# A fused attention, mixture-of-experts and dense kernel: attention paced ahead of the MoE, unsplit probabilities in the first chunk, the third MoE run backwards through its weights

## Chip, cores and metric

The kernel runs on one core of one Trainium2 chip. The metric is the device time of one execution in microseconds; lower is better. Engines are named as in the profile: PE is TensorE, DVE is VectorE, ACT is ScalarE, POOL is GpSimd, SP is the engine on which every DMA of this kernel is issued.

## What is computed

```python
# q, k, v: 2 batches, 8 heads, 768 positions, 64 wide; proj: 64 x 6
q_bucket, k_bucket = sign bits of q @ proj, k @ proj      # 6 bits make a bucket
scores = where(q_bucket == k_bucket, q @ k.T / 8, -1e9)
attn = softmax(scores) @ v                                # per batch and head
x = attn, heads side by side                              # 1536 tokens x 512
p = domain_probs / sum(domain_probs)
moe = sum over 4 experts e of p[:, e] * (relu(x @ w1[e]) @ w2[e])   # 512 -> 1024 -> 512
h = moe @ w_in                                            # 512 -> 1024
solu = h * softmax(h)
ln = (solu - mean) / sqrt(var + 1e-6) * g_ln
out = ln @ w_out                                          # 1024 -> 512
```

w_in, w_out and g_ln follow the inputs' double precision; the kernel decodes w_in and w_out from 64-bit words on the chip.

## The kernel before

The 1536 tokens are cut into four chunks of 384 (three tiles of 128). Chunks 0 and 1 belong to batch 0, chunks 2 and 3 to batch 1. For each chunk there is an attention (8 heads with 3 rows of 128 queries each) and a MoE of 32 slots; slot s has an A step (`moe_a`, L1312: 12 products of 384 columns against w1) and a B step (`moe_b`, L1363: 9 products of 512 columns against w2). At the end `dense` (L1453) does the last part for twelve tiles.

Precision is got by splitting: a value becomes a high and a low part, and a product is done as three. In the first chunk's attention and MoE the parts are f32r (a reduced fp32), later fp16. Weights arrive by DMA in `wra` (w1) and `wrb` (w2), 512 KB each, and are split into `wsa`, `wsb` by one instruction on ACT, DVE or POOL and one on DVE (`Stream.split`, L1245). Every chunk loads and splits all 16 + 16 pieces again; from the second chunk on the split parts go round a ring of 4 pairs for each kind (`ws16_r`, L521).

The first chunk's attention (`attn_first`, L937) stands alone at the start. Heads 0 to 5 normalise each row of probabilities, split it (`xh`, `xl`, `t`, `hha`, `hxa`) and multiply both parts with both parts of v: 12 f32r products for a head. Heads 6 and 7 (`h >= FH`) are *full*: probabilities are neither normalised nor split, transposed as they are into fp32 tiles (`ln`, `y`), multiplied in 6 fp32 products with a v tile (`wrb`) whose other half is ones, so that the sums come out beside the result, and divided afterwards (`av_out`, ratio, L906).

The attention of chunk c+1 (`attn_steps`, L1124) is mixed into the MoE of chunk c. A row (L1141 to L1153) does scores on PE, the maximum on DVE, the exponential on ACT (`p<-PS,sm`), scaling, a split into `hl`, and a DMA transpose into `t` or `t320h`; after three rows `av_mm` multiplies with v and `av_out` makes the chunk's input `xh`, `xl`. The first chunk of a batch also projects all k of that batch (`proj_steps(c, True)`, L1128), which takes the place of 9 steps. `Fill` (L1518) hands out steps by a rate per slot: chunk 1 in 22 slots, then, restarted two slots before each MoE's end, 31 slots for chunk 2 (50 steps, the k projection among them) and for chunk 3 (41 steps).

The program is recorded first. What is then issued is set by three tables: `ORDER` (which recorded operation comes next, over all engines), `FORMS` (which engine takes an operation that has a choice) and `BANKS` (which PSUM bank). `Recorder.emit` (L383) follows them; nothing is decided at run time, and each engine takes its instructions in that order.

Of the kernel before, what the change touches and what calls it, by code (L numbers as in the profile page):

```python
# [401 lines left out]
def lsh_attention_moe_solu(  # L402
# [17 lines left out]
    R = S // 128  # L420
# [14 lines left out]
    NR = 16  # L435
    LQ = 2 * D + NR
    LW = 128

    LA = 2
    GS = 2  # L440
    FH = 6
    LD = 1
    LB = 3
    DI = 2
    BM, BS, BE, BQ = 100, 150, 100, 50
    OUT0 = 4
    DBOOST = 0
# [473 lines left out]
    def x_tiles(c):  # L921
# [3 lines left out]
        if c:  # L925
            xT[c] = lower
# [591 lines left out]
    class Fill:  # L1518
# [6 lines left out]
        def start(self, c, slots):  # L1525
            for _ in self.it:
                pass
# [83 lines left out]
```

## Time and profile before

| | |
|---|---|
| time, median of 3 runs | 879.75 us (876.97 to 881.87) |
| the profiled execution's own time | 878.72 us |
| its span, first to last instruction | 876.6 us |
| PE busy | 832.7 us, 95% |
| DVE, ACT, POOL busy | 715.3, 489.6, 306.5 us |
| chain that ended last | PE 70%, DVE 9%, DMA 9%, issue 4%, ACT 3%, POOL 3% |
| DMA | 180.42 MB, mean 206 GB/s |

The profile gives, for one execution, when each engine was busy and what ended its idle time. All operations go through one recording helper, so nearly all stand under one line, L397; groups are told apart by the names of the tiles that they write and read (`out<-in`). A busy PE need not be PE at its peak, and the granted clock of PE is listed beside it.

### The profile page before, as it was taken

What the parts mean: (1) busy time and instruction counts of PE and PEld (TensorE: products, weight loads), DVE (VectorE), ACT (ScalarE), POOL (GpSimd) and SP (SyncE); (2) the same over time, 40 slices, a digit from 0 to 9 for tenths busy, and PEclk for the clock granted to TensorE, in tenths of its full rate; (3) what the DMA queues carried; (4) which work ended last, traced back from release to release, by engine and by line L of the source; (5) the groups of instructions that cost most, each with busy time, mean ns of one, the idle gap of its engine ahead of it and who ended that gap; (6) DMA issues with size and microseconds to landing.
All of it is one profiled execution on the core that took longest, in us unless ns stands there. A gap on an engine that the chain in (4) does not pass through costs nothing.

```text
span 876.6 us, 13313 instructions
## 1 busy us (share of the span) xinstructions
PE 832.7 (95%) x4431; PEld 531.4 (61%) x4431; DVE 715.3 (82%) x1476; ACT 489.6 (56%) x894; POOL 306.5 (35%) x325
## 2 busy tenths in 40 slices
PE   6789999999999999999769999999999999999997
PEld 5677789888886555655435555555555555444443
DVE  7978767877888978889978788887888889999872
ACT  4878547676795333667853566586344534443431
POOL 1645552545533131244512243543433221111220
PEclk9999999999999999999969999999999999999999
DMA  7986766998999798899998799999477857234643
GB/s 193 261 202 180 222 205 140 229 238 211 243 241 290 249 261 245 204 268 230 227 191 265 181 277 233 252 242 215 145 248 206 253 194 248 67 80 79 125 97 96
DMA packets 250069, 180.42 MB, mean 206 GB/s; under 512 B 166673, under 2 KB 218257, under 8 KB 250001
## 3 DMA queue, kind: packets, MB, share of 16 engines
q1 hardware_dynamic: 250000, 179.58, 79.4%
q8 instruction: 35, 0.57, 0.3%
q14 instruction: 34, 0.27, 0.1%
HBM read 116.10 MB, written 19.73 MB: 155 GB/s over the span
## 4 chain that ended last, share of the span: by engine, by line
PE 70%; DVE 9%; DMA 9%; issue 4%; ACT 3%; POOL 3%; SPq 1%; POOLq 0%; DVEq 0%; ACTq 0%
PE PS L397 70%; DMA t<-hl 5%; ACT p L397 2%; DVE sm L397 2%; DMA t320h<-hl 1%; POOL hl L397 1%; SPq L397 1%; DVE hl L397 1%; DVE st L397 1%; DVE p L397 1%; DMA wrb<-in_moe_w_dram 1%; DVE ln L397 1%; DVE wsa0h L397 1%; DVE xp L397 0%; DMA qB<-qD 0%
## 5 line engine op out<-in xcount | busy, mean ns | idle before, releaser
L397 ACT ACTIVATE p<-PS,sm 128x768 f32<-128x768 f32 x96 | 94.9, 989 | 34.9 <-DVE sm L397 16.8
L397 DVE TENSOR_REDUCE sm<-PS 128x1 f32<-128x768 f32 x96 | 90.8, 950 | 20.2 <-PE PS L397 19.1
L397 PEld LDWEIGHTS <-wsa1h 128*128 128x128 f16 x576 | 55.7, 98 | 42.1 <-issue 3.7
L397 PEld LDWEIGHTS <-wsa0h 128*128 128x128 f16 x576 | 55.6, 98 | 39.8 <-issue 1.6
L397 POOL TENSOR_SCALAR sm<-sm 128x1 f32<-128x1 f32 x97 | 34.3, 355 | 107.3 <-DVE sm L397 52.4
L397 PE MATMUL PS<-xh,wsa 128*128 128x384 f32 x256 | 68.8, 336 | 0.0
L397 PE MATMUL PS<-kB,qB 80*128 80x384 f32 x192 | 66.1, 344 | 2.0 <-DMA qB<-wsb 1.4
L397 PE MATMUL PS<-xh1h,wsa1h 128*128 128x384 f16 x256 | 67.0, 326 | 0.9 <-DVE y L397 0.9
L397 PE MATMUL PS<-xh1h,wsa0h 128*128 128x384 f16 x256 | 66.7, 326 | 0.0
L397 ACT ACTIVATE hha0h<-PS 128x384 f16<-128x384 f32 (+1 forms) x66 | 31.9, 489 | 58.4 <-PE PS L397 55.7
L397 POOL TENSOR_TENSOR hl<-p,hl 128x768 f16<-128x768 f32 x25 | 42.6, 1704 | 58.1 <-DVE hl L397 28.6
L397 PEld LDWEIGHTS <-hha0h 128*128 128x128 f16 x400 | 36.8, 98 | 40.5 <-issue 3.7
L397 PE MATMUL PS<-kC,qC 128*128 128x384 f32 x144 | 56.1, 390 | 5.0 <-ACT p L397 4.8
L397 PE MATMUL PS<-wsb0h,hha0h 128*128 128x512 f16 x200 | 59.7, 380 | 0.0
L397 PE MATMUL PS<-wsb1h,hha0h 128*128 128x512 f16 x200 | 59.6, 380 | 0.0
L397 DVE TENSOR_TENSOR hl<-p,hl 128x768 f16<-128x768 f32 x47 | 45.7, 973 | 10.1 <-ACT hl L397 5.1
L397 ACT ACTIVATE p<-p,sm 128x768 f32<-128x768 f32 x47 | 43.6, 931 | 15.9 <-DVE sm L397 15.6
L397 POOL TENSOR_SCALAR ln<-ln 128x512 int32<-128x512 int32 x21 | 23.9, 1136 | 77.0 <-DVE ln L397 69.7
L397 PEld LDWEIGHTS PS<-xh,wsa 128*128 128x128 f32 x256 | 46.6, 188 | 0.4
L397 DVE SCALAR_TENSOR_TENSOR hxa0h<-PS,hha0h 128x384 f16<-128x384 f32 x64 | 34.8, 550 | 10.2 <-ACT hha0h L397 10.1
L397 PE MATMUL PS<-xl,wsa 128*128 128x384 f32 x128 | 43.0, 336 | 0.0
L397 PE MATMUL PS<-wsb,hha 128*128 128x512 f32 x132 | 41.9, 398 | 0.0
(303 smaller groups left out, 2292.7 us busy)
## 6 DMA issues: line engine op xcount, KB each, us to landing
wra<-in_moe_w_dram SPq DMA_DIRECT2D x64, 512.0 KB, 5.1
wrb<-in_moe_w_dram SPq DMA_DIRECT2D x64, 512.0 KB, 4.7
kC<-kD SPq DMA_DIRECT2D x24, 384.0 KB, 4.4
vr<-in_v_dram SPq DMA_DIRECT2D x30, 192.0 KB, 4.0
kB<-kD SPq DMA_DIRECT2D x24, 240.0 KB, 4.8
qD<-stk SPq DMA_DIRECT2D x27, 192.0 KB, 3.2
qC<-qD SPq DMA_DIRECT2D x24, 192.0 KB, 3.9
ln<-in_moe_w_in_dram SPq DMA_DIRECT2D x8, 512.0 KB, 4.5
```

The source lines that it names most:

```text
L397: fn(**{key: self.now(x) for key, x in kw.items()})
```

## The change

- `FULL` holds all eight heads: in the first chunk no probability is normalised or split. The full heads' transposed probabilities now go to the `t` tiles and v to the `hl` (fp16) tiles read as fp32. `av_out` copies the numerators to `xp` and divides two heads at once, on odd heads.
- The k projection of batch 1 moves from the head of chunk 2's attention to the tail of chunk 1's.
- `Fill` follows one table of ends: chunk 1's q projection and attention by slot 22, both projections for chunk 2 by slot 32, chunk 2's attention by slot 55, all of chunk 3's by slot 89 of the first 96.
- The third MoE takes its weights in reverse. The split parts of the last six pieces of each kind stay in SBUF, and the next MoE's first six are those: 6 loads and splits of each kind fewer in the third MoE, and as many in the fourth. The ring grows to 6 pairs; the two new ones lie in `ln` and `ee`.
- The decoding of w_in and w_out begins at slot 4 of the last MoE and is spread to slot 30, since it uses `ln`.
- `ORDER`, `FORMS` and `BANKS` are new throughout.

```diff
 ORDER = """
-3 13 0 1 0 10 28 14 21 14 1 19 9 22 18 9 0 0 16 2 0 15 8 0 26 11 11 12 19 5 10 2 10 9 5 0 12 7 3 12 3 9 5 9 8
...
-    FH = 6
+    FULL = (0, 1, 2, 3, 4, 5, 6, 7)
...
+    x = cuts(ln_r.t[0], 1024) + cuts(ee_r.t[0], 1024)
+    for i in (1, 2):
+        j = 4 * (i - 1)
+        ws16_r[i].t = [(x[j], x[j + 1]), (x[j + 2], x[j + 3])] + ws16_x[i]
...
         if ratio:
             acopy(tmp[m, 0:N], ps[l0:l0 + 64, 0:N], bias=1e-9)
-            V.reciprocal(out=tmp[m, 0:N], in_=tmp[m, 0:N])
-            V.tensor_tensor(out=xp[m, 0:N], in0=ps[m, 0:N], in1=tmp[m, 0:N], op=ALU.mult)
+            copy_by("AV", xp[m, 0:N], ps[m, 0:N])
+            if h % 2 == 1:
+                V.reciprocal(out=tmp[:, 0:N], in_=tmp[:, 0:N])
+                sub_by("VG", xp[:, 0:N], xp[:, 0:N], tmp[:, 0:N], ALU.mult)
...
-            full = h >= FH
+            full = h in FULL
...
     def attn_steps(c):
-        if r0 == 0:
-            yield from proj_steps(c, True, None, a_b, pp_b, stk_r)
...
+        if c + 1 < NC and chunks[c + 1][1] == 0:
+            yield from proj_steps(c + 1, True, None, a_b, pp_b, stk_r)
...
         def split(self, i):
+                if self.ns in self.again:
+                    self.spl[self.ns] = self.spl[self.again[self.ns]]
...
+    KEEP = 6
+    def turned(c, x):
+        return x[::-1] if c == 2 else x
...
+            if c > 1 and len(W1.items) - i1["m", c, turned(c, range(NP))[0]] < KEEP:
+                W1.again[len(W1.items)] = i1["m", c - 1, m]
...
     class Fill:
-        def start(self, c, slots):
...
+        ends = ((NS - 10, H + 1 + H * (NT + 1)), (NS, 2 * H + 2), (2 * NS - 9, H * (NT + 1)), (3 * NS - 7, H + 1 + H * (NT + 1)))
...
-            if c == NC - 1 and s % DI == 0:
+            moe_b(c, s)
+            if c == NC - 1 and s > 3 and (s - 4) * 16 // 26 > (s - 5) * 16 // 26:
                 next(dec_it, 0)
```

The tables' effect shows in the order of instructions. Three places follow, all on PE. The first is head 0's product with v in the first attention (`vs` is v, `wsa,wsb` and `kB,qB` are scores, `idn,p` transposes of probabilities). Before:

```order
L397 MATMUL PS<-kB_126,qB_128 128x384
L397 MATMUL PS<-xh_94,vs_74 128x384 x4
L397 MATMUL PS<-hha_108,vs_74 128x384 x2
L397 MATMUL PS<-xl_96,vs_74 128x384 x4
L397 MATMUL PS<-hxa_110,vs_74 128x384 x2
L397 MATMUL PS<-idn,p_77 128x128 x4
```

With the change (`t` holds the probabilities, `hl` holds v):

```order
L389 MATMUL PS<-kB_126,qB_128 128x384
L389 MATMUL PS<-idn,p_79 128x128 x4
L389 MATMUL PS<-idn,p_77 128x128 x6
L389 MATMUL PS<-t_82,hl_80 128x384 x6
L389 MATMUL PS<-wsa_104,wsb_106 128x384
```

Twelve f32r products became six fp32 products. The second place is the end of batch 1's k projection (`idr,hl` transposes k, `stk,lhs_w` projects it). Before, it is among products of the second MoE (`xh1h,wsa1h`, fp16):

```order
L397 LDWEIGHTS hxa0h
L397 MATMUL PS<-wsb0h,hxa0h 128x512
L397 MATMUL PS<-stk_66,lhs_w 128x384 x2
L397 LDWEIGHTS wsa1h
L397 MATMUL PS<-xh1h,wsa1h 128x384
```

With the change it is among B steps of the first MoE (`wsb,hhb`, f32r):

```order
L389 MATMUL PS<-wsb_106,hhb_109 128x512 x2
L389 MATMUL PS<-wsb_106,hxb_111 128x512
L389 MATMUL PS<-idr,hl_65 128x128 x3
L389 MATMUL PS<-stk_67,lhs_w 128x384 x2
L389 MATMUL PS<-wsb_106,hhb_109 128x512 x2
L389 MATMUL PS<-wsb_106,hxb_111 128x512
L389 MATMUL PS<-stk_66,lhs_w 128x384 x2
```

The projection moved ahead of the whole second MoE. The third place is the end of chunk 2's attention (`t83,vs1h` and `t320h,vs2h` are products with v of heads 5 and 6, the rest is chunk 3's q projection). Before, no product of a MoE stands between them:

```order
L397 MATMUL PS<-t_83,vs1h 128x384
L397 MATMUL PS<-idr,hl_65 128x128 x3
L397 MATMUL PS<-idr,hl_64 128x128 x3
L397 MATMUL PS<-stk_66,lhs_w 128x384
L397 MATMUL PS<-stk_67,lhs_w 128x384
L397 MATMUL PS<-idr,hl_65 128x128 x3
L397 LDWEIGHTS vs2h
L397 MATMUL PS<-t320h,vs2h 128x384
```

With the change, behind head 6's product, B steps of the second MoE (`wsb0h,hha0h`) are still to be done:

```order
L389 MATMUL PS<-t320h,vs2h 128x384
L389 MATMUL PS<-stk_66,lhs_w 128x384
L389 MATMUL PS<-idr,hl_64 128x128 x3
L389 MATMUL PS<-idr,hl_65 128x128 x3
L389 LDWEIGHTS hha0h
L389 MATMUL PS<-wsb0h,hha0h 128x512
L389 LDWEIGHTS hha0h
L389 MATMUL PS<-wsb0h,hha0h 128x512
```

Work of the second MoE was all issued ahead of these products; now some of it is left for PE while the last heads finish, ahead of the third MoE's first product.

## Rows read from the trace of the kernel before

**Rows 1.** The page: span, and part 1, busy time of each engine.
```profile
span 876.6 us, 13313 instructions
PE 832.7 (95%) x4431; PEld 531.4 (61%) x4431; DVE 715.3 (82%) x1476; ACT 489.6 (56%) x894; POOL 306.5 (35%) x325
```

**Rows 2.** Busy time by stage: stretch, length, engines' busy us (instructions), PE clock, DMA, GB/s.
```profile
16.90:95.50 78.60, 66.07 (x374) 54.33 (x372) 66.76 (x140) 61.39 (x136) 41.28 (x70) 0.98 0.79 215
95.50:270.40 174.90, 172.74 (x918) 151.72 (x917) 135.17 (x247) 117.02 (x215) 85.83 (x73) 1.00 0.84 216
270.40:426.50 156.10, 154.03 (x856) 88.36 (x856) 133.43 (x245) 83.97 (x151) 50.44 (x56) 1.00 0.95 252
426.50:462.20 35.70, 22.10 (x106) 14.51 (x106) 28.01 (x55) 21.72 (x47) 11.25 (x17) 0.76 0.92 199
462.20:621.60 159.40, 157.76 (x866) 90.76 (x866) 130.37 (x238) 95.66 (x166) 60.04 (x57) 1.00 0.97 234
621.60:747.60 126.00, 126.00 (x682) 66.56 (x680) 109.78 (x187) 57.52 (x98) 34.98 (x27) 1.00 0.70 219
747.60:876.60 129.00, 124.22 (x580) 56.68 (x578) 99.56 (x341) 44.67 (x70) 19.36 (x13) 1.00 0.40 88
```

**Rows 3.** Waits of PE from 426 to 463 us: total, times, longest.
```profile
PE PS L397 <- DVE xp L397: 5.2, 1, 5.2
PE PS L397 <- ACT p L397: 4.4, 2, 2.8
PE PS L397 <- DMA qD<-stk: 2.5, 1, 2.5
```

**Rows 4.** Groups: the exponential in 270.4:426.5, 426.5:462.2, 462.2:621.6 (x is rows).
```profile
L397 ACT ACTIVATE p<-PS,sm 128x768 f32<-128x768 f32 x17 | 16.8, 987 | 4.2 <-POOL sm L397 2.3 <-DVE sm L397 1.6
...
L397 ACT ACTIVATE p<-PS,sm 128x768 f32<-128x768 f32 x7 | 6.9, 987 | 0.1
...
L397 ACT ACTIVATE p<-PS,sm 128x768 f32<-128x768 f32 x24 | 23.7, 987 | 13.0 <-DVE sm L397 9.1 <-POOL sm L397 1.8 <-DVE hxa0h L397 1.7
```

**Rows 5.** Timeline of PE at 79 us: start, length, instruction, count.
```profile
79.56 2.25 PE L397 MATMUL PS<-t,vs 128*128 128x384 f32 x12
81.64 4.03 PE L397 MATMUL PS<-ln,wrb 128*128 128x384 f32 x12
85.51 2.33 PE L397 MATMUL PS<-idn,p 128*128 128x128 f32 x18
```

**Rows 6.** Waits of PE from 16.9 to 95.5 us: total, times, longest.
```profile
PE PS L397 <- POOL p L397: 3.4, 5, 1.0
PE PS L397 <- ACT p L397: 3.1, 6, 1.1
...
PE PS L397 <- DVE hxa L397: 0.9, 1, 0.9
...
PE PS L397 <- ACT sm L397: 0.6, 1, 0.6
PE PS L397 <- DVE xl L397: 0.6, 1, 0.6
```

**Rows 7.** Groups in 16.9:95.5: busy, mean ns, idle time before.
```profile
L397 POOL TENSOR_SCALAR p<-p,sm 128x768 f32<-128x768 f32 x12 | 10.9, 906 | 9.4 <-DVE sm L397 8.5 <-PE PS L397 0.7
...
L397 DVE TENSOR_TENSOR xl<-PS,xh 128x512 fp32r<-128x512 f32 x9 | 6.1, 682 | 0.1
...
L397 DVE RECIPROCAL tmp<-tmp 64x384 f32<-64x384 f32 x2 | 5.1, 2547 | 1.3 <-ACT tmp L397 1.3
```

**Rows 8.** The page: a weight's second split; a load of w1 and its landing.
```profile
L397 DVE SCALAR_TENSOR_TENSOR wsb1h<-wrb,fit,wsb1h 128x1024 f16<-128x1024 f32 x26 | 35.2, 1356 | 3.4 <-POOL wsb1h L397 1.9 <-ACT wsb1h L397 1.4
...
wra<-in_moe_w_dram SPq DMA_DIRECT2D x64, 512.0 KB, 5.1
...
t<-hl SPq DMA_TRANSPOSE x48, 4.8
```

More of the change, by code (lines that the diff above doesn't have):

```diff
@@ L23 @@
 ORDER = """
[106 rows of a table removed]
[99 rows of a table added]
 """
 FORMS = """
-AGVVGVAGAVVVVAAVAAVAAVVAVAAAAAGAGGAVVVVAGAAGAAGAVAVGAGAGAGGGAGAGAGAAAAGGGAGAGAGVAGAGAAGGGGGVGAGAAVGAAAVVAAAGVA
-AGGVGAAVAVGGAAGAGVAAGVVGGAAAVVGAAAGGAAGGAGVVGVGAGAVAVVAGVAGAVVAVAAVVGGGGVGAGVGAVVAVAAGVAGAGAGAGAAGAAGGVVGVAAVA
-GGGAVGVGAAVAVVVGVVAVGAAVAGVGVVVAGGAGVVAVGAVAVAVAVAAVAVVGVVVAGAGGVAVGVGAVAGGAVAVGVAVAVVAGVAAVVVAVGAGAGVGVVGAAVG
-AAAGGAGVAAVAVAAVVVAGGAVVVGGGAAGVVGVAVVAGVVAVAVAVGVAAGVAGAGAAVAVGVGAAVGAVGGGGAGVAAVAVAAVAVGVVGVGGAGVAGAVVVVAGVG
-AVAGVVAGAVVGVVAGAVAVVGAVVAAVAAGGVAGVAVVAVVAAVVAAGGVGAVAAGAVVAAAAVGAGGAVGAAVAGGVAAVVGVVAVVAVAVAAGAVVVVAVVVGGGGG
@@ L138 @@
-GGVAAGGAAAAGVGAGVVVVGAAVGAAVVAVVAGVVVAVAVAGAAGAGVVVAAAAVGVAGGVVAGGAAAGVAGAVVAAVVGVAVGAGVAGAGVVAVAGAAAAAVGVGVVG
-VGAVGVGVVAGVAGAAVAVAVVAVGAGAGGGAGGAGAVAGAGGVAAGAAAAGGAGAVAGVAAAGGAVGAVVAVAVAGGGVAGVAAVVAVVVAGVVVVVAAGVAGVVVVAV
-VAVAVVVVAAVVVGVVGVVAVVVAVVAGGAGGGVAGVVAAGAAVVVGVVAVAGAVVVVVAAVAVVAAGGVAAGAGAVVVAVVVAAVVAAVGGAAVAGVGVGVAAGGVVGG
-AGGGGVGGGAVAVGGVAAAVAGAGVGVVVGAVVVAAAAAGGVVVAVVGGAAGAGVAGVAGAGVAAAAAGVAGGVVVAVVAAVVAGAGGAAGVAVVVVAVVVAGAVGAGVV
-GGAAGAVVVAVAAGAGVAAGAAVAVAVGGAAVAAAGGAAAAVAAVVVGAAAVAAGGVAAAAAVAAVAAVAGAGGGAVVAVVGAVAAVVGGAGAAGVVVAGGGAVAVVAVA
@@ L143 @@
-A
+GVAVAAVVVAAVAAVAAVAGAAAVVAAAAAVVGAVAAAVVAGAVGVAGVAVAVVVAVAVAGGAVGGVGVAGVGGAVAAVVVAAAGAGAAVVVAAVVVGVVVVGAGVAAAG
+GVGAVAVVAAAGAVVVVGAAGAVGVGVAVGVGAAVVGGVVGGAAGVAVAVAAAVVAVVAVVVAVAAVVAVAAGVVGGGVAVAAVVAGGVVGAAVAVGVAGAAAVGVAVAA
+GGAVVVVAVVVAVGAGAAVGVAGAAAVAGVAAGVGVVVVVAAGVVAVVAVAAVGAAVVVAGGAAAGVGVGAAAGVVAAVAGVVGAGVAAVAAVAAVAVVAAGAAVGVAGA
+GVGAAVVAGAVAGVAGVAAVGVAGVAGVVAVAVGAAVAGVAVAGAGVAVGAAGAVAGAGVVGVAVGVAVAGAGVAGVVGVAAGAGVGVVAGAGVVGGAVAVAVAVGVAGA
+GVGVAGAAGVAAAVVAVVGAGVAVAVAVGAVVVVVVGVVVVAGAGVGVAAAGAGVAAGAGGGGAAVGAAAAVVVAAVAAVAAGAAGAAAAAGVAGAVGVVVAAAGGAVVV
@@ new lines @@
+AVGAGVGGAVGVAVVVGAAAAGGAAVGAGGAAAVGAGVVGVAAGAVAVAGVVAGAGVVGGVVVAAVVAGGVVAVAAGGAGGAAVAVVAGAVAGVGGGAAGAAGVGGGAVA
+GGVAVVVVAAVAVVVGAGVVAVAGVAGVGVGVVGAGAGGAAVVVVGAGAAAVGVAAVGAVVGVVGAVGGVGGGGVGVAVVAVVAGAVVVGAGAGAGVGGGAGAGAGGGGG
+VGGVVAGAAVAVGVAGAGGVGVVGVAGVVAVVAGGGGAGVGVAAGVAVGVGVGGVVAAVGVVAGVAGVVVAGAGVGGVVGAVVGGVAGGAVAGAGVAAVAGVGAGVAGAV
+VAAVVAGVGGAVAAVVGGAGAGVVAGGVVGVAAAAVGVAVVVGVVGVVGGVAVGVGVVVVVAGAAGGAAAGVVAVAVAAGAVVVGAVAAAVAGGAAVAAAAVGAAAAVAA
+AVAAVAVAVAVAAVGAAAVVVGAAAVVVGAGGGVAAAGAGVAGVGVAAVAA
@@ L144 @@
 """
 BANKS = """
-73062064160357612045050120461040726540235742036431020136124061234163021423610432613401423612010263704250767216
-03076234651436521065324635645635634513240365757436446362030621455364346453753763467621321301270231630127367676
-37451340273524574375462146340635634634656103621406346564367464206410204600234523406753213640356456420345731634
-63636513046210367537436436034231607351254735647574325702540143041623673541702645656450135645620546026340326342
-630162410
+52174372354027165406053217317503741604530215626304121064013063464210601241647203606234102360142010754604712147
@@ L152 @@
+54102447536564365401620546345346537546320164326573563543463536346546402163767373637337667376363763653672047163
+73344365436365312065435736543463261452103754357466353655456036214046343674646377365630241635345345450357436521
+36565734634356021403643634534636346561256452012707123653246124130462423534120657205264763545642106462343063206
+235161043
 """
@@ L520, in lsh_attention_moe_solu @@
     hh16_r, hl16x_r = (Ring(0, tiles=cuts(t[1], TM) + cuts(t[0], TM)) for t in (hh_t, hx_t))
-    ws16_r = {}
+    ws16_r, ws16_x = {}, {}
     for i in (1, 2):
@@ L524, in lsh_attention_moe_solu @@
         ws16_r[i] = Ring(0, tiles=[(x[a][2 * j], x[a][2 * j + 1]) for j in range(2) for a in range(2)])
+        ws16_x[i] = ws16_r[i].t
     y_r = Ring(1, [128, NT, DM], F32, "y")
@@ L561, in sub, with sub_by @@
         eng.tensor_tensor(out=out, in0=a, in1=b, op=ALU.subtract)
-    def sub_by(names, out, a, b):
-        rec.add([(name, "tensor_tensor", dict(out=out, in0=a, in1=b, op=ALU.subtract)) for name in names])
+    def sub_by(names, out, a, b, op=ALU.subtract):
+        rec.add([(name, "tensor_tensor", dict(out=out, in0=a, in1=b, op=op)) for name in names])
     def ops_by(names, out, in_, a, b, op0, op1):
@@ L654, in fit_v @@
     def fit_v(b):
-        ts = [t.rearrange("p a r q -> p (a r q)").bitcast(F32)[:, 0:H // 2 * R * D] for t in t16_r.t[0:2]]
+        if b:
+            ts = [t.rearrange("p a r q -> p (a r q)").bitcast(F32)[:, 0:H // 2 * R * D] for t in t16_r.t[0:2]]
+        else:
+            x = ln_r.t[0].rearrange("p a n -> p (a n)")
+            ts = [x[:, i * H // 2 * R * D:(i + 1) * H // 2 * R * D] for i in range(2)]
         for i, t in enumerate(ts):
@@ L921, in x_tiles @@
     def x_tiles(c):
-        xT[c] = x = (xh_r.next(), xl_r.next())
-        lower, upper = (tuple(flat16(t)[:, i * KD * TM:(i + 1) * KD * TM].rearrange("p (k q) -> p k q", k=KD) for t in x) for i in range(2))
-        yT[c] = upper if c < 2 else lower
-        if c:
-            xT[c] = lower
+        x = (xh_r.t[0 if c in (0, 3) else 1], xl_r.t[0 if c in (0, 3) else 1])
+        lower, upper = (
+            tuple(flat16(t)[:, i * KD * TM:(i + 1) * KD * TM].rearrange("p (k q) -> p k q", k=KD) for t in x) for i in range(2)
+        )
+        xT[c], yT[c] = {0: (x, upper), 1: (lower, lower), 2: (upper, upper), 3: (lower, lower)}[c]
     def row(U, rr, sb, E, pr_=p_r):
@@ L1023, in attn_first @@
         vs_f = Ring(0, tiles=vs_r.t[0:2])
-        vp = [t.rearrange("p a n -> p (a n)")[:, 0:S].rearrange("p (r a d) -> p r a d", r=R, a=2) for t in wr_r[2].t]
+        vp = [t.rearrange("p a n -> p (a n)").bitcast(F32).rearrange("p (r a d) -> p r a d", r=R, a=2) for t in hl16_r.t]
         for hi, t in enumerate(vp):
@@ L1043, in unit @@
             hi = h % 2
-            if h >= FH:
+            if h in FULL:
                 vs = vp[hi]
@@ L1065, in attn_first @@
         )
-        cut = lambda x: x.rearrange("p (m q) -> p m q", q=N)
-        fdst = Ring(
-            0,
-            tiles=[
-                [[cut(kf[:, 0:KD * N])], [cut(kf[:, KD * N:R * N])]],
-                [[cut(qf[:, 0:KD * N])], [cut(kf[:, R * N:2 * R * N - KD * N])]],
-            ],
-        )
+        fdst = [t.rearrange("p a r q -> p (a r q)").bitcast(F32).rearrange("p (r q) -> p r q", r=R) for t in t16_r.t[0:2]]
+        fdst = Ring(0, tiles=[[[t[:, 0:KD]], [t[:, KD:R]]] for t in fdst])
         U = unit(0)
@@ L1229, in __init__ @@
             self.of = {}
+            self.again = {}
+            self.tile = {}
             self.nl = 0
@@ L1239, in load @@
             while self.nl <= min(i, len(self.items) - 1):
+                if self.nl in self.again:
+                    self.nl += 1
+                    continue
                 t = self.as_item(wr_r[self.kind].next(), self.nl)
@@ L1246, in split @@
             while self.ns <= min(i, len(self.items) - 1):
+                if self.ns in self.again:
+                    self.spl[self.ns] = self.spl[self.again[self.ns]]
+                    self.tile[self.ns] = self.tile[self.again[self.ns]]
+                    self.ns += 1
+                    if self.ns not in self.again:
+                        ring = ws16_r[self.kind]
+                        ring.t = [self.tile[i] for i in range(self.ns - KEEP, self.ns)]
+                        if self.of[self.ns][0] == NC - 1:
+                            ring.t = [t for t in ring.t if any(t is x for x in ws16_x[self.kind])]
+                        ring.n = 0
+                    continue
                 self.load(self.ns)
@@ L1250, in split @@
                 if c:
-                    w = ws16_r[self.kind].next()
+                    self.tile[self.ns] = w = ws16_r[self.kind].next()
                     w = [x.rearrange("p (a n) -> p a n", a=t.shape[1]) for x in w]
@@ L1271, in lsh_attention_moe_solu, with slot @@
     i1, i2 = {}, {}
+    NP = NS // 2
+    KEEP = 6
+    def turned(c, x):
+        return x[::-1] if c == 2 else x
+    def slot(c, s):
+        return NS - 1 - s if c == 2 else s
     def add_moe1(c, lo, hi):
-        for m in range(lo, hi):
+        for m in turned(c, range(lo, hi)):
             e, fp = divmod(m, NF // 2)
             i1["m", c, m] = len(W1.items)
+            if c > 1 and len(W1.items) - i1["m", c, turned(c, range(NP))[0]] < KEEP:
+                W1.again[len(W1.items)] = i1["m", c - 1, m]
             W1.of[len(W1.items)] = c, m
@@ L1280, in add_moe2 @@
     def add_moe2(c, lo, hi):
-        for m in range(lo, hi):
+        for m in turned(c, range(lo, hi)):
             e, fp = divmod(m, NF // 2)
             i2["m", c, m] = len(W2.items)
+            if c > 1 and len(W2.items) - i2["m", c, turned(c, range(NP))[0]] < KEEP:
+                W2.again[len(W2.items)] = i2["m", c - 1, m]
             W2.of[len(W2.items)] = c, m
             W2.items.append(w2[e][fp * 256:fp * 256 + 256, :].rearrange("(k p) f -> p k f", p=128))
-    NP = NS // 2
     for c in range(NC):
@@ L1312, in moe_a @@
     def moe_a(c, s):
-        m, j = divmod(s, 2)
+        m, j = divmod(slot(c, s), 2)
         i = i1["m", c, m]
@@ L1331, in moe_a @@
         hT["m", c, s] = split_h(ps, N, True, c == 0)
-        if j == 0:
+        if s % 2 == 0:
             W1.split(i + 1)
@@ L1350, in lsh_attention_moe_solu, with y_update @@
     y_t = {}
-    def y_update(c, e, t):
+    def y_update(c, at, e, t):
         b, r0, n = chunks[c]
@@ L1355, in y_update @@
         g = pr[:, b * R + r0 + t, e:e + 1]
-        if e == 0:
+        if at == 0:
             if t == 0:
@@ L1361, in y_update, with moe_b @@
             V.scalar_tensor_tensor(out=y_t[c][:, t], in0=o, scalar=g, in1=y_t[c][:, t], op0=ALU.mult, op1=ALU.add)
-    def moe_b(c, s, more=0):
+    def moe_b(c, s):
         n = chunks[c][2]
-        parts = []
-        for x in range(s, s + more + 1):
-            m, j = divmod(x, 2)
-            parts.append((x, W2.get(i2["m", c, m]), hT.pop(("m", c, x)), j))
-        for tiles in [[t] for t in range(n)] if more else [range(n)]:
-            for x, w, (hh, hl), j in parts:
-                e, fi = divmod(x, NF)
-                mm2(("m", c), tiles, hh, hl, w, j, fi == 0, fi == NF - 1)
-            if fi == NF - 1:
-                for t in tiles:
-                    y_update(c, e, t)
-                    if e == E - 1:
-                        y_fit(c, t)
-        m, j = divmod(s + more, 2)
-        i = i2["m", c, m]
-        if j == 0:
+        m, j = divmod(slot(c, s), 2)
+        i = i2["m", c, m]
+        hh, hl = hT.pop(("m", c, s))
+        at, fi = divmod(s, NF)
+        mm2(("m", c), range(n), hh, hl, W2.get(i), j, fi == 0, fi == NF - 1)
+        if fi == NF - 1:
+            for t in range(n):
+                y_update(c, at, slot(c, s) // NF, t)
+                if at == E - 1:
+                    y_fit(c, t)
+        if s % 2 == 0:
             W2.split(min(i + 1, i2["out", 0] - 1))
@@ L1518, in lsh_attention_moe_solu, with __init__, __call__ @@
     class Fill:
-        it = iter(())
-        rate = 0.0
-        due = 0.0
-        def start(self, c, slots):
-            for _ in self.it:
-                pass
-            if c < NC:
-                b, r0, n = chunks[c]
-                self.it = attn_steps(c)
-                self.rate = ((H + 1) * (2 if r0 == 0 else 1) + H * (n + 1)) / slots
-            self.due = 0.0
-        def __call__(self, w=1.0):
-            self.due += self.rate * w
-            while self.due >= 1.0:
-                self.due -= 1.0
+        ends = ((NS - 10, H + 1 + H * (NT + 1)), (NS, 2 * H + 2), (2 * NS - 9, H * (NT + 1)), (3 * NS - 7, H + 1 + H * (NT + 1)))
+        def __init__(self):
+            self.it = (x for c in range(1, NC) for x in attn_steps(c))
+            self.at, self.done = 0, 0
+        def __call__(self):
+            self.at += 1
+            due = first = 0
+            for end, steps in self.ends:
+                due += steps * min(1.0, max(0.0, (self.at - first) / (end - first)))
+                first = end
+            while self.done < int(due + 1e-6):
+                self.done += 1
                 next(self.it, 0)
@@ L1553, in lsh_attention_moe_solu @@
     W2.split(0)
-    fill.start(1, NS - 10)
     for c in range(NC):
@@ L1559, in lsh_attention_moe_solu @@
         for s in range(NS):
-            if s == NS - LA and c + 1 < NC:
-                fill.start(c + 2, NS - 1)
             a_to(c, s + LA + 1)
@@ L1564, in lsh_attention_moe_solu @@
                 a_to(c + 1, s + LA + 1 - NS)
-            fill()
-            if c == NC - 1 and s % DI == 0:
+            if c < NC - 1:
+                fill()
+            moe_b(c, s)
+            if c == NC - 1 and s > 3 and (s - 4) * 16 // 26 > (s - 5) * 16 // 26:
                 next(dec_it, 0)
-            moe_b(c, s)
-            if c == NC - 1 and s == 17:
+            if c == NC - 1 and s == 18:
                 fit_norm(dm[:, 0:8].unsqueeze(1), NM, WA)
```

204 rows, old and new, of the table ORDER are left out of this document.

## Prediction

> **What bounds the kernel now.** I read the page first: PE is busy for 832.7 of 876.6 us, more than any other engine [rows 1]. So the time is PE's work plus the 43.9 us in which PE waits, and an edit counts only if it changes one of the two. Next I cut the span where PE's work changes its kind [rows 2]: the first attention (16.9 to 95.5), the four MoEs (to 270.4, 426.5, then 462.2 to 621.6, and 747.6) and the dense end. The reader is to compare the first number of a row, its length, with the second, PE's busy time. In the second and third MoE rows and in the last MoE they nearly agree: 154.03 of 156.10, 157.76 of 159.40, 126.00 of 126.00. Two rows stand out. The first attention leaves 78.60 - 66.07 = 12.5 us idle. The stretch from 426.5 to 462.2 leaves 35.70 - 22.10 = 13.6 us idle, and there PE's granted clock averages 0.76: it fell from 2.4 to 1.2 GHz for part of the stretch, after its longer idle times, so the same products also took longer.
>
> What is that stretch? It lies between the second MoE's last product and the third MoE's first. The waits [rows 3] name `xp`, `p` and `qD`, all tiles of the attention. The count of exponentials tells how late that attention is [rows 4]: of chunk 2's 24 rows, 17 were done by 426.5 and 7 were left. The third MoE needs all of them. PE has nothing but these rows and chunk 3's q projection to do, and the row chain (maximum, exponential, split, DMA transpose) sets the pace, 35.7 / 7 = 5.1 us for a row. I call the stretch the hole.
>
> **The change, part by part.**
>
> *Attention paced ahead, k projection moved.* If chunk 2's attention ends before the second MoE does, the hole's products lie beside MoE products that are needed anyway. The hole's real work is PE's busy time at full clock: 22.10 x 0.76 = 16.8 us. What goes is 35.7 - 16.8 = 18.9 us. Does it end in time? The third MoE's stretch held 24 rows in 159.4 us with 1.6 us idle [rows 2, 4], 6.6 us a row. The second MoE's stretch gets longer by the hole's work, 156.1 + 16.8 = 172.9 us, less the k projection, which goes to the first MoE; I count some 165 us, in which 24 rows at 6.6 us need 159. That fits, with little to spare, and only because the projections are over when the second MoE begins, as the second place of the order shows. The k projection's loads, stores and transposes go to a stretch with a DMA share of 0.84 instead of 0.95, DVE 77% busy instead of 85% [rows 2]; PE's work in it only changes place, so it costs nothing in the sum. On SP its 8 loads and 8 stores now queue among chunk 1's last transposes, where a late one would delay chunk 1's last rows; MoE work lies behind those, so I charge nothing there. What is late next is the tail of chunk 2: in the new order head 7's product with v has only a few MoE products around it, and a transpose lands 4.8 us after its issue [rows 8]. The nearest wait of that kind took 5.2 us [rows 3]. Bounds are 0 and 5.2 us; nothing speaks for either end, so I take about the middle, 2.5 us.
>
> *Unsplit probabilities.* Six heads go from 12 f32r products to 6 fp32 products. The timeline has both next to each other [rows 5]: 12 f32r products from 79.56 to 81.64 are 2.08 us; 6 fp32 products, shown as 12 records, from 81.64 to 85.51 are 3.87 us. Each head costs PE 1.79 us more, six heads 10.7 us, on the path. The records go at 3.87 / 12 = 0.32 us, so one fp32 product takes 0.645 us. The Trainium skill (FP8 and Floating Point Precision, section TensorE Precision Notes) says that true fp32 takes four passes through the array. By that rule an fp32 product would be four f32r products, 4 x 2.08 / 12 = 0.69 us, and the six heads would cost 6 x (4.16 - 2.08) = 12.5 us. By the rows it is 3.87 / 2.08 x 2 = 3.7 f32r products, so the trace does not quite agree, and the measured 10.7 us stands in the sum.
>
> What it gives back is waits. The removed work is the scaling of 18 rows (906 ns each on POOL), the second copies of the split (682 ns for the larger half on DVE), the split of v, and the row reciprocals [rows 7]. It adds numerator copies and two more reciprocals of 2547 ns (four in place of two, for two heads each) [rows 7]. DVE, ACT and POOL were busy for 66.8, 61.4 and 41.3 us of the 78.6 [rows 2]; none is the bound alone, but PE waited for just these instructions. Of PE's waits those on POOL's `p` (3.4 us), on `hxa` (0.9), `xl` (0.6) and the row scale `sm` (0.6) lose their cause, and about half of those on ACT's `p` (3.1), which is both scaling and exponential [rows 6]: 3.4 + 0.9 + 0.6 + 0.6 + 1.5 = 7.0 us. Bounds: 0, if scores and loads come last instead, and 12.5, all of the idle time. A head's fp32 products also cover 3.87 us of the next rows' chain, which is why I do not go below 7.
>
> *The third MoE backwards.* 24 loads of 512 KB and 24 splits go: 24 x 1.36 = 33 us of DVE and about as much on ACT and POOL, and 24 x 0.5 MB of DMA [rows 8]. I charge nothing for it. In both stretches in which it falls PE was busy for all but 1.6 us [rows 2], so it is off the path; it helps only as slack for the attention's tail. If the cover went, one split of 1.36 us would show at a time. The decoding starts four slots later, as it needs `ln`, and its 16 steps go at the same pace over the same MoE; behind it PE has 126.0 of 126.0 us of its own, and the decode of w_in has still to be over before the dense part. Zero again; above it, at most one step's delay, 126 / 16 = 7.9 us; a gain is excluded since PE is full there.
>
> *Sum.* 876.6 + 10.7 - 7.0 - 18.9 + 2.5 = 863.9 us of span. The profiled execution took 878.72 us for a span of 876.6, 2.1 us more: 866.0 us. It lies 1.0 us under the median of the runs shown, 879.75, well inside their spread, so I leave it at that.
>
> **The rivals.**
>
> *The hole only shrinks* (no change). The row chain in the second MoE needs more than the 6.6 us of the third, since the stretch also ends the projections and reads with a DMA share that was 0.95 already. A delay of 0.4 us a row is 24 x 0.4 = 10 us of hole. Against it: the 7 rows in the hole went at 5.1 us. Time: 866 + 10 = 876 us.
>
> *The chain stays behind PE* (slower). If a row of chunk 2 takes 7.4 us or more beside a full MoE, with one transpose stream, one SP queue and DVE at 85%, the third MoE begins some 24 x 0.8 = 19 us late: the hole is back in full, in whatever place, and the fp32 products are still paid. Time: 866 + 19 = 885 us. It decides at 7.2 us a row, where 24 x 0.6 = 14 us eat up the gain. For it speaks that the order is fixed by tables and one late transpose holds the SP queue for all; against it the 24 rows at 6.6 us in the third MoE with the same engines.
>
> *The first attention becomes PE's own* (faster still). If the long fp32 products hide the whole row chain, all 12.5 us of idle time return and the tail of chunk 2 is covered: 876.6 + 10.7 - 12.5 - 18.9 + 2.1 = 858 us. For it speaks that every side engine loses work; against it that PE there also waited for the loads of `qB` and the exponential, which stay.
>
> *It does nothing that it says* is excluded for the places shown: the order has them moved.
>
> **How the numbers follow.** The forecast (hole closed, part of the first waits returned, 861 to 871 us) gets 0.62, the faster rival 0.16, the shrunken hole 0.15, the slower one 0.07. The likeliest is 866 us. The range goes from 857, just below the faster rival, to 876, the shrunken hole; with no waits returned and the 5.2 us tail the sum is 876.6 + 10.7 - 18.9 + 5.2 + 2.1 = 875.7 us, also its end. A measurement of this kernel can tell about 0.5%, 4.4 us, from no change. Faster than 875.4: 0.62 + 0.16 and a third of the shrunken hole, 0.83. Within: 0.11. Slower than 884.1: 0.06.
>
> **What would show it.** Right: no stretch of over 6 us with PE idle between the second and third MoE; clock 1.00 there; 24 exponentials before the second MoE's last product; fp32 products at 0.32 us a record and the first attention some 4 us longer. Wrong: PE waits on `xp`, `hl` or `t` for over 10 us around the third MoE's start; the first attention over 10 us longer; a new wait on `ln` or on weights at the start of the last MoE or of the dense end.

## The result and the profile after

The changed kernel takes 866.82 us (median of 4 runs, 864.93 to 867.72) against 879.12 us before (now of 4 runs): a ratio of 0.986, 95% interval 0.982 to 0.989. It is faster by 1.4%, clear of the noise, and 866.0 us had been forecast. The profiled execution took 864.93 us for a span of 863.0 us. The page after, span and part 1, against [rows 1]:

```profile
span 863.0 us, 13106 instructions
PE 835.2 (97%) x4431; PEld 528.6 (61%) x4431; DVE 666.6 (77%) x1387; ACT 471.1 (55%) x862; POOL 274.8 (32%) x302
```

PE is busy for 2.5 us more and idle for 16.1 us less: 863.0 - 835.2 = 27.8 us, where it was 876.6 - 832.7 = 43.9. By stage (columns as in [rows 2]; the second MoE's first product is at 276.2 us, the third's at 438.8, the fourth's at 601.1, the dense part's at 724.5):

```profile
16.50:96.70 80.20, 72.75 (x368) 53.34 (x367) 56.83 (x96) 52.76 (x112) 18.57 (x34) 1.00 0.78 211
96.70:276.20 179.50, 178.07 (x958) 155.88 (x957) 144.93 (x263) 127.11 (x238) 81.78 (x76) 1.00 0.90 243
276.20:438.80 162.60, 159.19 (x895) 93.60 (x894) 136.59 (x263) 100.33 (x184) 64.39 (x76) 1.00 0.96 241
425.00:455.00 30.00, 30.00 (x171) 17.52 (x170) 21.50 (x40) 9.65 (x20) 8.02 (x14) 1.00 0.48 128
438.80:601.10 162.30, 160.23 (x874) 91.59 (x873) 117.10 (x217) 80.45 (x145) 58.66 (x69) 1.00 0.75 178
724.50:863.00 138.50, 131.39 (x611) 59.76 (x609) 105.60 (x354) 50.94 (x80) 18.73 (x13) 1.00 0.43 100
```

The fourth line is the place where the hole was: PE is busy for all 30 us at a clock of 1.00, where [rows 2] had 22.1 of 35.7 us at 0.76. The third MoE now starts 11.3 us before the second one's last product ends at 450.1 us. The exponential's group in 276.2:438.8 has all of chunk 2's rows ([rows 4] had 17):

```profile
L389 ACT ACTIVATE p<-PS,sm 128x768 f32<-128x768 f32 x24 | 23.7, 986 | 12.2 <-DVE sm L389 5.8 <-POOL sm L389 4.8 <-POOL hl L389 1.0
```

The first attention has 80.20 - 72.75 = 7.45 us of idle PE, where [rows 2] had 12.5, and 6.7 us more of PE's work. Its waits: `POOL p`, `hxa`, `xl` and `sm` are gone as forecast, while those on ACT's `p` grew from 3.1 us [rows 6] to 4.7:

```profile
PE PS L389 <- ACT p L389: 4.7, 8, 1.0
PE PS L389 <- DMA wsa<-wsa: 1.0, 1, 1.0
PE PS L389 <- DVE xp L389: 0.5, 1, 0.5
```

The timeline of PE shows the six fp32 products (12 records) of two heads, and what follows each:

```profile
65.25 4.04 PE L389 MATMUL PS<-t,hl 128*128 128x384 f32 x12
69.12 1.84 PE L389 MATMUL PS<-idn,p 128*128 128x128 f32 x14
...
72.20 4.03 PE L389 MATMUL PS<-t,hl 128*128 128x384 f32 x12
75.78 0.63 PE L389 MATMUL PS<-wsa,wsb 128*128 128x384 f32 x1
```

From the first start to the last end a head takes 4.03 to 4.04 us, as it did before (4.03 in [rows 5]), and the records follow each other every 0.32 us. From start to the next group's start it is 3.87 us where transposes follow and 3.58 us where a score follows, but that score's record is then 0.63 us long, where one behind another score is 0.34 us: it begins before the fp32 products end. So 3.58 us is no shorter product.

### The profile page after: what moved, and what is told of

Read it like the earlier page. It is cut to its first block, busy times and chain, and to the rows that moved or that the text cites. A ratio compares the mean times of both kernels' runs of the same rounds, so it can differ in the third digit from the quotient of the medians.

```text
span 863.0 us, 13106 instructions
## 1 busy us (share of the span) xinstructions
PE 835.2 (97%) x4431; PEld 528.6 (61%) x4431; DVE 666.6 (77%) x1387; ACT 471.1 (55%) x862; POOL 274.8 (32%) x302
## 4 chain that ended last, share of the span: by engine, by line
PE 71%; DVE 13%; DMA 7%; ACT 4%; issue 2%; SPq 2%; POOL 1%; ACTq 0%; DVEq 0%; POOLq 0%
PE PS L389 71%; DVE sm L389 3%; DVE ln L389 2%; ACT p L389 2%; DVE st L389 2%; DMA t<-hl 2%; SPq L389 2%; DMA qD<-stk 1%; DVE hl L389 1%; DMA xh1h<-hl 1%; POOL sm L389 1%; DMA wra<-in_moe_w_dram 1%; DMA xl0h<-hl 1%; DVE tmp L389 1%; DVE t L389 1%
## 5 line engine op out<-in xcount | busy, mean ns | idle before, releaser
L389 DVE TENSOR_REDUCE sm<-PS 128x1 f32<-128x768 f32 x96 | 90.8, 950 | 22.1 <-PE PS L389 20.8
L389 POOL TENSOR_SCALAR sm<-sm 128x1 f32<-128x1 f32 x95 | 38.7, 408 | 155.0 <-DVE sm L389 93.6
L389 POOL TENSOR_TENSOR hl<-p,hl 128x768 f16<-128x768 f32 x30 | 52.6, 1754 | 32.0 <-ACT hl L389 22.4
L389 PEld LDWEIGHTS <-wsa1h 128*128 128x128 f16 x408 | 39.3, 98 | 31.0 <-issue 3.4
L389 PEld LDWEIGHTS <-wsa0h 128*128 128x128 f16 x408 | 39.4, 98 | 28.1 <-issue 0.9
L389 DVE TENSOR_TENSOR hl<-p,hl 128x768 f16<-128x768 f32 x42 | 43.0, 1024 | 12.7 <-ACT hl L389 9.6
L389 PE MATMUL PS<-xh1h,ln 128*128 128x384 f16 x192 | 50.5, 326 | 0.8 <-DVE y L389 0.8
L389 PE MATMUL PS<-wsb0h,hha0h 128*128 128x512 f16 x164 | 48.9, 380 | 0.0
L389 PEld LDWEIGHTS <-ln 128*128 128x128 f16 x336 | 32.1, 98 | 23.9 <-issue 2.2
L389 PE MATMUL PS<-wsb1h,hha0h 128*128 128x512 f16 x152 | 45.3, 380 | 0.0
L389 PE MATMUL PS<-xh1h,wsa1h 128*128 128x384 f16 x160 | 42.2, 326 | 1.7 <-ACT p L389 1.7
```

The source lines that it names most:

```text
L389: fn(**{key: self.now(x) for key, x in kw.items()})
```

## The experiments

The change has three parts that were undone one by one or done alone. Every instruction's place is in tables, so each mixed kernel needed a table of its own. That was the difficulty: three ways of writing tables were tried, each with a control, and an untuned table costs from nothing to 17%. So the totals are read with care, and the question whether the hole is there is read from the stages.

The three undoings, as diffs against the changed kernel. **S**, split again in heads 0 to 5:

```diff
-    FULL = (0, 1, 2, 3, 4, 5, 6, 7)
+    FULL = (6, 7)
...
-            copy_by("AV", xp[m, 0:N], ps[m, 0:N])
-            if h % 2 == 1:
-                V.reciprocal(out=tmp[:, 0:N], in_=tmp[:, 0:N])
-                sub_by("VG", xp[:, 0:N], xp[:, 0:N], tmp[:, 0:N], ALU.mult)
+            V.reciprocal(out=tmp[m, 0:N], in_=tmp[m, 0:N])
+            V.tensor_tensor(out=xp[m, 0:N], in0=ps[m, 0:N], in1=tmp[m, 0:N], op=ALU.mult)
```

**F**, the third MoE forwards, nothing kept, decoding as before:

```diff
-        ws16_r[i].t = [(x[j], x[j + 1]), (x[j + 2], x[j + 3])] + ws16_x[i]
+        ws16_r[i].t = ws16_x[i]
...
-    KEEP = 6
+    KEEP = 0
...
-        return x[::-1] if c == 2 else x
+        return x
...
-        return NS - 1 - s if c == 2 else s
+        return s
...
-            moe_b(c, s)
-            if c == NC - 1 and s > 3 and (s - 4) * 16 // 26 > (s - 5) * 16 // 26:
+            if c == NC - 1 and s % DI == 0:
                 next(dec_it, 0)
+            moe_b(c, s)
...
```

**P**, the old pace and the k projection at its old place:

```diff
     def attn_steps(c):
+        if r0 == 0:
+            yield from proj_steps(c, True, None, a_b, pp_b, stk_r)
...
-        if c + 1 < NC and chunks[c + 1][1] == 0:
-            yield from proj_steps(c + 1, True, None, a_b, pp_b, stk_r)
...
     class Fill:
-        ends = ((NS - 10, H + 1 + H * (NT + 1)), (NS, 2 * H + 2), (2 * NS - 9, H * (NT + 1)), (3 * NS - 7, H + 1 + H * (NT + 1)))
+        it = iter(())
+        rate = 0.0
+        due = 0.0
...
```

All results, each ratio to the kernel before. The stage columns come from the starts and ends of PE's instructions in the profiled execution, in us: the start of the first MoE; the second MoE's stretch, from its first product to the third's first; from the second MoE's last product to the third's first (negative: they overlap); and from the second MoE's first product to the first scores of chunk 2.

```
run                    undone   ratio, 95%              1st MoE  2nd MoE   gap    rows start
before                 S F P    -                          95.5    191.8    35.7     80.0
changed kernel         -        0.986 (0.982 to 0.989)     96.7    162.6   -11.3     22.2
f000_control           S F P    1.001 (0.998 to 1.003)     96.0    192.2    36.1     80.0
f001_pace_alone        S F      1.108 (1.102 to 1.115)    109.0    188.9   -11.3     27.7
f010_backwards_alone   S P      1.092 (1.086 to 1.098)    101.7    220.4    35.8    104.1
f100_unsplit_alone     F P      1.010 (1.007 to 1.013)    106.0    190.8    35.3     80.0
g111_control           -        1.152 (1.148 to 1.155)    118.1    203.9   -10.6     30.3
g110_old_pace          P        1.178 (1.173 to 1.182)    127.2    219.3    42.0     90.0
g101_forwards          F        1.180 (1.175 to 1.184)    119.7    219.9   -12.3     31.5
g011_split             S        1.156 (1.151 to 1.161)    117.1    204.0   -10.6     29.3
h111_control           -        1.015 (1.012 to 1.017)    101.7    171.4   -11.3     27.5
k101_forwards          F        1.021 (1.016 to 1.025)    102.9    168.4   -11.8     28.0
k011_split             S        0.999 (0.997 to 1.000)    105.2    165.2   -11.4     27.3
k111_k_late            k late   1.036 (1.034 to 1.039)    102.1    197.9   -10.6     77.7
```

**One part alone** (f). The tables take each instruction at its measured start in one of the two kernels. The control:

> The kernel before once more, with its order written out by the same procedure that makes all the mixed kernels (each instruction placed by its measured start), and the two fp32 heads in the buffers of the changed kernel. All theories: 0.997 to 1.003 of the kernel before, 876 to 882 us, with the hole of PE between second and third MoE (at about 426 to 462 us, some 19 us of PE waits). If it is off by more, the mixed kernels can't be read.

It came out at 1.001, 36.1 us from MoE to MoE.

> Only the new pace and the moved k projection; probabilities split, third MoE forwards. Theory 1 (the pace closes the hole): 863 to 867 us, ratio 0.982 to 0.987, under 3 us of PE waits between second and third MoE, 24 exponentials in the second MoE's stretch. Theory 2 (the attention keeps up only because the third MoE backwards takes 24 weight splits and 24 loads from DVE and DMA): a hole of 8 us or more stays, 871 to 880 us. Theory 3 (the gain is the unsplit probabilities' relief of POOL and DVE): 876 to 882 us.

> Only the third MoE backwards with six weights kept of each kind, and the decoding four slots later; probabilities split, the old pace. Theory 1: 877 to 881 us, ratio 0.997 to 1.003, hole as before, though 24 loads and 24 splits are gone. Theory 2: 864 to 872 us, since the hole shrinks to under half. Theory 3: 877 to 881 us.

> Only the unsplit probabilities in all heads of the first chunk; old pace, third MoE forwards. Theory 1: the first attention 1 to 4 us longer and nothing else, 879 to 884 us, ratio 1.000 to 1.005, hole as before. Theory 2: as theory 1. Theory 3: 865 to 873 us.

The totals missed: the first two by far (975 and 959 us), with PE waits all over the program, which I lay to their tables; the third, 887.58 us, by 4 us. But the stages answer the question. Busy time between the second and third MoE, with the pace alone:

```profile
495.00:530.00 35.00, 32.62 (x183) 18.52 (x182) 28.18 (x46) 12.81 (x23) 12.27 (x15) 1.00 0.59 165
```

with the weights backwards alone:

```profile
482.40:518.20 35.80, 22.63 (x105) 14.98 (x104) 26.06 (x53) 21.43 (x46) 6.20 (x15) 0.71 0.98 216
```

and with the unsplit probabilities alone:

```profile
437.40:472.70 35.30, 22.59 (x104) 14.80 (x103) 28.14 (x55) 21.55 (x47) 11.26 (x17) 0.76 0.95 209
```

The last two have the hole of [rows 2] almost to the instruction, with the 5.2 to 5.3 us wait on `xp` too; with the pace it is gone, even in a kernel that is 11% slower. Theory 1 holds for the hole; theories 2 and 3 fall for it. What f001 does not show is the time won: its second MoE takes 188.9 us to the third's first product, nearly the 191.8 us before, so the time went elsewhere in that stretch.

**One part undone** (g). The tables come from a list procedure that gives each engine one instruction at a time.

> The changed kernel with nothing undone, its order written anew by the list procedure that now makes the mixed kernels (durations and landing times of the traces, one instruction at a time on each engine, ties by the measured start). The mixed kernels of the first procedure spread PE waits over the whole program, so this is the control for the second. All theories: ratio 0.980 to 0.992, 862 to 872 us, no hole between second and third MoE. If it is over 0.995, the second procedure costs too much to read the others at 1%; they are then read against this run and not against the changed kernel.

> The changed kernel with only the old pace and the k projection at its old place; probabilities unsplit, third MoE backwards. Theory 1 (the pace closes the hole): 10 to 18 us slower than the control of this procedure, the PE waits of some 10 us or more and a granted clock under 1 between second and third MoE are back. Theory 2 (the third MoE backwards lets the attention keep up): within 5 us of the control, no hole. Theory 3 (unsplit probabilities give the gain): within 5 us of the control.

> The changed kernel with only the third MoE forwards again: 24 more weight loads and 24 more splits; pace and unsplit probabilities stay. Theory 1: within 4 us of the control, under 3 us of PE waits between second and third MoE. Theory 2: 8 us or more over the control, with PE waits on weights (wsa, wsb tiles) or on rows of the attention in the second or third MoE. Theory 3: within 4 us.

> The changed kernel with only the probabilities of the first six heads split again (12 f32r products instead of 6 fp32 ones, scaling before the product). Theory 1: 0 to 4 us faster or slower than the control: about 9 us of PE work saved in the first attention (1.5 us a head by the trace of the changed kernel) against some 5 to 8 us of PE waits on scaling and splits that come back. Theory 2: as theory 1. Theory 3: 8 us or more slower than the control.

The control alone stood at 1.152: the procedure had counted a transfer as done once it was issued. By its own terms the totals can't be read at 1%: g110 and g101 are 23 and 24 us over this control, which would speak for theories 1 and 2 at once, and g011 is 3.5 us over it. The stages repeat the finding: a gap of 42.0 us with the old pace and none in the other three, whatever else is undone. Busy time in the gap of g110:

```profile
535.90:577.90 42.00, 24.20 (x105) 14.94 (x104) 26.03 (x48) 19.15 (x38) 16.80 (x29) 0.73 0.90 222
```

This holds for the gap alone: the second MoE's whole stretch is 219.3 us in g110 and 219.9 us in g101, 15 and 16 us over the control's 203.9, so in these tables F, which also takes the ring's two new pairs from the second MoE, lengthens that stretch as much as the old pace does.

**A better control** (h). The same procedure, with the landings counted.

> The changed kernel with nothing undone, its order written by a third procedure. The second one had left out that a transfer lands some 3 to 8 us after its issue, one behind the other; the third one counts each landing in one line behind the last, with a margin. All theories: the ratio is 0.975 to 0.995 if transfers were what the second procedure missed, and over 1.05 if it was something else; then no mixed kernel of these procedures can be read.

It came to 1.015, between the two ranges and 26 us over the changed kernel. Counting the landings took 119 us off (1011.71 to 892.78 us); what the rest is stays open. One difference is seen on the pages: this table chooses engines anew and puts 364 instructions on POOL (g111: 359), the changed kernel 302.

**F again**, by that procedure, but with the engines of the changed kernel nearly kept:

> The changed kernel with only the third MoE forwards again: 24 more weight loads and 24 more splits; pace, k projection and unsplit probabilities stay. Order by the third procedure, now with each instruction kept on the engine that it has in the changed kernel or moved between DVE and ACT alone; its control stood 3% over the changed kernel, so up to 893 us are within the procedure's own cost. Theory 1 (the pace closes the hole, the weights backwards are off the path): 865 to 885 us, and whatever the total, under 5 us of PE waits between 430 and 470 us, chunk 2's 24 exponentials over before the second MoE's last product, clock 0.98 or more there. Theory 2 (the attention keeps up only because 24 splits and loads are gone): a hole of 8 us or more between second and third MoE or PE waits of 8 us or more on weight tiles in the third MoE, and 880 us or more.

```profile
430.00:470.00 40.00, 37.51 (x220) 21.99 (x219) 32.06 (x49) 18.83 (x37) 18.05 (x17) 1.00 0.94 231
```

PE waited 2.5 us in these 40, at clock 1.00, and no weight tile is among the waits. The total, 896.67 us, is above theory 1's range, but only 3.9 us over the control, and the two intervals touch. The control is not quite one: this table has 315 instructions on POOL, the control's 364, so a cost of F can hide behind the control's own. In the second MoE, which loses the ring's two new pairs, F costs nothing against the control: 168.4 us against 171.4. The 24 loads and splits fall in the third and fourth MoE. In the fourth they are off the path, as predicted: 123.4 us to the dense part's first product in this kernel, the control and the changed one. In the third it is less plain: PE is idle for 7.1 of 168.6 us, against 4.2 of 167.2 in the control and 2.1 of 162.3 in the changed kernel. No weight tile is among PE's waits there, but DVE is busy for 146.3 us and not for the control's 124.4. The dense part, from its first product to the end of the span, with F:

```profile
756.40:891.30 134.90, 130.98 (x611) 59.76 (x609) 105.21 (x342) 45.56 (x71) 19.56 (x13) 1.00 0.37 85
```

PE is idle for 3.9 us there, with no wait listed. In the control it is 7.7 us, and this wait for the exponential of a dense tile is the longest part:

```profile
PE PS L389 <- ACT PS L389: 3.8, 2, 3.2
```

The changed kernel has it too (2.6 us, 7.1 us idle); before, f000 and f100 have 4.8 us idle and no such wait. All eight kernels with the weights backwards have it, 1.7 to 6.7 us. That would put it down to the weights backwards and the later decoding, but f001 and g101, forwards both, have 6.3 and 4.8 us of it in their slow tables. So it isn't settled whether the part or the table makes it.

**S again**, kept close to the changed kernel's table:

> The changed kernel with only the probabilities of the first six heads split again, kept close to the changed kernel's order. Read at the start of the first MoE (96.7 us in the changed kernel, 95.5 before) and in the total. Theory 1 as predicted (fp32 products cost 10.7 us, waits returned 7.0): the first MoE starts 2 to 6 us earlier than in the changed kernel, total 861 to 868 us if the order costs nothing, up to 890 with the procedure's cost. Theory 3 (the unsplit probabilities relieve POOL and DVE so much that the new pace needs them): the first MoE starts no earlier, PE waits on scaling and splits of 8 us or more in the first attention, and the waits reach into the first MoE, where chunk 1's attention now has more to do.

877.73 us: the hole is closed and the gain is gone. The first MoE starts 8.5 us later than in the changed kernel. Busy time there:

```profile
17.00:105.20 88.20, 72.06 (x368) 59.75 (x367) 69.35 (x138) 62.90 (x137) 39.19 (x64) 0.88 0.75 201
```

and PE's longest waits:

```profile
PE PS L391 <- POOL p L391: 4.9, 6, 1.3
PE PS L391 <- ACT p L391: 3.7, 5, 1.4
PE PS L391 <- POOL hl L391: 1.8, 1, 1.8
```

The waits on POOL's scaling are back, 16.1 us of idle in all, and the clock fell to 0.88. Theory 1's earlier start is missed by 10 us or more, which looks like theory 3. Its third sign is missing: from the first MoE's first product to the second's there are 179.5 us, as in the changed kernel. And f100 is the mirror: unsplit probabilities in the old surroundings start the first MoE 10 us late as well (106.0 us), with a wait of 3.1 us on a transfer into `wsa`, a clock of 0.94 in the stretch, and one head's fp32 products at 6.41 us where most take 4.0. Both the kernel before and the changed one start the first MoE at 96 us, these two mixtures at 105 and 106. How much of that is the table and how much the part stays open.

**The k projection late** (k), against the same control as F:

```diff
     def attn_steps(c):
+        if r0 == 0:
+            yield from proj_steps(c, True, None, a_b, pp_b, stk_r)
...
-        if c + 1 < NC and chunks[c + 1][1] == 0:
-            yield from proj_steps(c + 1, True, None, a_b, pp_b, stk_r)
```

> The changed kernel with the k projection of the second half back at the head of chunk 2's attention, as before the change; chunk 2's rows are asked for as early as they can follow it, third MoE backwards and unsplit probabilities stay. The pace alone (theory 1a): projections follow each other faster, rows start by 325 us, the second MoE's stretch (its first product to the third's first, 162.6 us in the changed kernel, 171.4 in the control of this procedure, 191.8 before) stays under 176 us. The moved k projection is the lever (theory 1b): rows can't start before some 345 us, and the stretch grows to 185 us or more, as a hole or as waits in it; total 10 us or more over the control of this procedure (893 us).

The diff alone moves nothing. The changed kernel's `Fill` draws the steps of all chunks as one sequence, in which these nine stand between chunk 1's last head and chunk 2's q projection either way; in the change itself, too, it is `ends` and `ORDER` that put them early, not the place of the two lines. What the run changes is its table: both projections of chunk 2 now lie in the second MoE. Like F's, this table nearly keeps the changed kernel's engines (302 instructions on POOL in both), which the control's does not.

911.69 us, 18.9 over its control (892.78). That is theory 1b, as far as one table can tell. The second MoE's stretch, until the first scores of chunk 2 and after:

```profile
284.30:362.00 77.70, 61.73 (x333) 34.23 (x331) 49.53 (x88) 33.77 (x56) 15.04 (x18) 0.91 0.79 248
362.00:482.20 120.20, 114.28 (x635) 67.69 (x634) 102.67 (x192) 78.04 (x149) 55.87 (x68) 1.00 0.97 235
```

Though the rows were asked for as early as they can follow, they start at 362.0 us and not by theory 1a's 325, 77.7 us into the MoE, nearly as before (80.0), and PE waits 16 us while the two projections go on, most of it on the copies into `stk`. No hole stands between the MoEs; the time is lost inside the second one.

## Why the prediction was right, step by step

The total is right, and so is the step that carries it. The smaller terms were mis-sized on both sides; that they nearly cancel is luck. From the spans, 876.6 to 863.0, in us:

| step | predicted | measured |
|---|---|---|
| first attention: fp32 products | +10.7 | +10.5 at full clock |
| first attention: half clock gone, PE's other work | 0 | -3.8 |
| first attention: waits returned | -7.0 | -5.1 |
| the hole | -18.9 | -18.9 |
| tail of chunk 2 | +2.5 | 0 |
| weights backwards, later decoding | 0 | up to +2.3, at the dense end |
| not in the sum | 0 | +1.4, by difference |
| sum | -12.7 | -13.6 |

*The hole.* It went in full: 35.7 - 22.1 = 13.6 us of idle time and 22.1 - 16.8 = 5.3 us of lower clock. Both figures come from the rows before; what the runs add is that nothing of it is left. The step's reason is half right. The k projection is over when the second MoE begins, its last product at 267.5 us. The q projection behind it is not: its last product comes 13 us into the MoE, where before it came 69 us in:

```profile
289.22 0.44 PE L389 MATMUL PS<-stk,lhs_w 128*128 128x384 f32 x1
```

The margin was wider than it looked. The step counted 24 rows at 6.6 us, "with little to spare". Before, the rows themselves took 109 us from their first scores to the last head's product with v, 4.6 us each; they only started 80 us into the MoE, behind both projections. Now they start after 22.2 us and take 136 us, 5.7 us each. The late k projection shows, in its one table, that it is this start that counts. From the first scores to the third MoE there are 162.6 - 22.2 = 140.4 us now, 5.9 a row, where 4.6 had been reached: the rival *the chain stays behind PE* had less for it than the text said.

*The unsplit probabilities.* The products were sized right. All products with v keep PE busy for 32.4 us now. Before it was 15.2 us for six heads and 8.2 for two, 23.4 in all, and one head's f32r products ran at half clock there, 3.75 us instead of the 2.25 of [rows 5]:

```profile
59.89 3.75 PE L397 MATMUL PS<-t,vs 128*128 128x384 f32 x12
```

So the products cost 9.0 us more, and 9.0 + 1.5 = 10.5 us at full clock, for 10.7 forecast. What the sum lacked is that 1.5 us, and 2.3 us by which PE's other work in the stretch is shorter: 72.75 - 66.07 = 6.7 us more in all. Which work moved out and which lies closer wasn't traced. By the rule in the Trainium skill (FP8 and Floating Point Precision, section TensorE Precision Notes), four passes for true fp32, the estimate was 12.5 us. The trace after has the same 0.32 us a record as [rows 5], so 3.7 f32r products for an fp32 one, and does not quite agree with it either. The waits are the mis-sized term: 12.5 - 7.45 = 5.1 us came back and not 7.0. Those on scaling and splits went as named, but ACT's `p` did not give its half; it grew.

*The tail.* Head 7's product with v found its transposes landed: no wait of PE stands between 425 and 455 us. The lower bound was right.

*Weights backwards.* No gain shows where the step charged none: PE is idle for 2.1 us in the third MoE and for none in the fourth now, and was for 1.6 us and none with all loads and splits [rows 2]. What the step called zero may not be zero at the dense end: 7.1 us of idle PE against 4.8, with a new wait on a dense tile's exponential. The step had looked for a wait on `ln` or w_in. k101 lacks this wait but is idle longer in its third MoE, so whether the changed kernel with the third MoE forwards would beat both is open.

*What would show it.* No idle stretch between the MoEs, clock 1.00, 24 exponentials, 0.32 us a record: all there. The first attention is 1.6 us longer (80.20 against 78.60) and not 4; no wait on `xp`, `hl` or `t` stands around the third MoE's start.

## What to carry to other kernels

A hole at the end of a stage may be decided at its beginning: ask when the chain that fills it starts, and what stands in front of it, before asking how fast it goes. Here the rows went slower than before, 136 us against 109, and the hole still closed, since they began 22 us into the MoE and not 80. When parts of a tuned order are tested one by one, run a control of the ordering itself, with the same choice of engines, and read whole stages besides the totals. And measure a group of products to its own end: the next record can start before it.

## What the runs showed that was not expected

- The order and the engines of the same operations are worth 17%: 866.8 us in the changed kernel, 1011.7 in g111, 892.8 in h111. Between the last two the landings of transfers were counted, and the margins with them. In the changed kernel's trace all 571 transfers land in the order of their issue, in the kernel before a transpose into `t` 4.8 us after it [rows 8]; each engine takes its instructions in a fixed order, so one placed as if it could follow at once holds those behind it.
- In k011 16.1 us of idle time in the first attention came with a clock of 0.88, while 7.45 us, in waits of 1.0 us at most, left it at 1.00 in the changed kernel. The sum of idle time alone does not tell: f000 has 13.8 us of it there, in waits of 1.3 us at most, and a clock of 1.00.
